# Attention ahead of a routed expert layer: Q and K in two buffers, 25 held tiles, loads spread out, gate transposes moved, last products in other banks

## The chip, the cores and the metric

The kernel runs on one core of one Trainium2 chip. The metric is the device time of one execution in microseconds; the numbers shown for a kernel are the median of several executions and their range. The core has a matrix engine (TensorE, PE in the profile; its weight loads are PEld), a vector engine (VectorE, DVE), a scalar engine (ScalarE, ACT), a general one (GpSimd, POOL) and a queue engine that issues transfers (SyncE, SP). Each engine runs its own instructions in the order in which the program was written and waits for the others through semaphores. Matrix products land in PSUM, eight banks; everything else lies in SBUF.

## The reference

Windowed attention with heads, and then a mixture of experts in which every expert takes exactly its share of the tokens:

```
B, H, S, D = 8, 8, 576, 64
scores = (q @ k.transpose(0, 1, 3, 2)) / sqrt(D)
mask = (rel >= 0) & (rel < 64)               # rel = row - column
scores = where(mask, scores, -1e9) - max
attn = exp(scores); attn /= attn.sum() + 1e-9
x = (attn @ v).transpose(0, 2, 1, 3).reshape(B * S, H * D)   # 4608 x 512
...
logits = x @ w_gate                          # 4608 x 8
for idx in argsort(-logits.flatten()):       # highest first
    token, expert = idx // 8, idx % 8        # token free and expert under 576: it goes there
...
out[mask] = relu(x[mask] @ w1[e]) @ w2[e]    # 512 -> 1024 -> 512 for each expert
```

## The kernel before, in words

There are three stages: attention (the first 157 us or so), the routing of the first expert (to about 183 us, a search on DVE and PE), and the experts, which fill PE to the end. All instructions behind the attention stand in the same order in both kernels; the change touches the function `attention` and nothing else.

The 4608 rows are worked through in 36 units of 128 rows, that is two blocks of 64 queries each. A batch has nine blocks, so units 0 to 4 touch batch 0, 4 to 8 batch 1, and batch b begins in unit 9b//2. Step s of the main loop (the last loop of the function) writes down, in this order: the score products of unit s (`qk`, L133, PE) and their masking and row maximum (L142, DVE, eight instructions), the subtraction of the maximum (L149, POOL); the transposes of unit s-1 (`tr`, L155, PE, two groups of four heads) and their exponentials (L157, ACT); the products with V of unit s-2 (`pv`, L176, PE), a small copy of the row sums (L206, ACT), and on DVE the reciprocal (L207), the gate logits (L191) and the values (L201) (`norm`). Whatever the table `at` holds for step s comes last.

That table holds the gate work. The logits x @ w_gate are not made from x: V @ w_gate is made for each batch in two parts (blocks 0 to 3 and 4 to 8) and appended to V as eight columns. For each part there are the gate products (`gate_mm`, L88, PE), the gate copy out of PSUM (`gate_cp`, L92, ACT), the gate transposes (`gate_tr`, L98, PE) and the copies into V (`gate_out`, L104 and L107, ACT). After that come the even copies (`even`, L119, ACT): V shifted by 64 rows, two instructions for each of four tiles of a batch, needed because a block of 64 queries sees 128 keys that may begin in the middle of a tile of V.

PSUM: scores have four tiles of one bank each (`SP`), `bank()` hands out two banks in turn to gate products, gate transposes and each group of score transposes, and products with V have two (`po`). So a group of score transposes waits until the bank that was handed out two turns earlier has been read by ACT.

SBUF and transfers: Q and K have three buffers each, V with its columns (`VO`) three, the transposed V (`VT`) and the shifted one (`VE`) two. SP issues the loads of batches 0 and 1 at once, and in step (9(b-2)+5)//2 those of batch b: VT, Q, K, V, in that order. A load waits for the last reader of its buffer. The values of a unit lie in a ring of HOLD + 4 tiles until they are stored to `xs` in HBM; HOLD (16) and LOADED say how many are held back, and from which step two go out per step.

Of the kernel before, what the change touches and what calls it, by code (L numbers as in the profile page):

```python
# [9 lines left out]
FT = mybir.dt.float32  # L10
# [11 lines left out]
HP = H // 2  # L22
E = 8
WARM = 30
VW = 73
DM = H * D
HOLD = 16
LOADED = 9 * (B - 3) + 12


def attention(ctx, tc, c, q, k, v, vt, gate, xs, L, choices, setup, counters):
# [9 lines left out]
    SP = [[ps.tile([128, 2, 128], FT, name=f"Sp{r}{i}", bufs=1) for i in range(2)] for r in range(2)]  # L41
# [22 lines left out]
    def load_qk(b, i0, i1, h=slice(0, HP), q2=nc.sync):  # L64
        if not i0 and not h.start:
            Q[b] = ld.tile([128, HP, S], FT, name="Q", bufs=3)
            K[b] = ld.tile([128, HP, S], FT, name="K", bufs=3)
        for q1, t, x in ((nc.sync, Q, q), (q2, K, k)):
            q1.dma_start(t[b][:, h, 64 * i0:64 * i1], x[b, h, :, 64 * i0:64 * i1].rearrange("h p s -> p h s"))
# [51 lines left out]
    PT_, ST, OP_ = {}, {}, {}  # L121

# [44 lines left out]
    def pv(m, g):  # L167
        Op = po.tile([128, 4, VW], FT, name="Op")
# [52 lines left out]
    def load_all(b):  # L221
        load_vt(b, *ALL)
        load_qk(b, *ALL)
        load_v(b, *ALL)

    n = 36
# [5 lines left out]
    for b in range(B):  # L232
        s0 = (9 * (b - 1) + (6 if b < 4 else 7)) // 2
        for i, s in zip(PARTS, ((0, 2), (3, 5))[b] if b < 2 else (s0, s0 + 2)):
            put(s, gate_mm, b, *i)
            put(s, gate_cp, b, *i)
            put(s + 1, gate_tr, b, *i)
            put(s + 1, gate_out, b, *i)
# [3 lines left out]
    for b in range(2, B):  # L242
        put((9 * (b - 2) + 5) // 2, load_all, b)
# [10 lines left out]

    for s in range(n + 2):
        if s < n:
            fs = [qk(s, g) for g in range(2)]
            for g in range(2):
# [4 lines left out]
                sm(s, g)  # L263
        if 1 <= s < n + 1:
            for g in range(2):
                tr(s - 1, g)
        if 2 <= s:
            for g in range(2):
                pv(s - 2, g)
            nrm = [norm(s - 2, g) for g in range(2)]  # L270
            for inv, gates, values in nrm:
                for f in (inv, gates, values) if s < n + 1 else (inv, gates):
                    f()
            if s >= n:
                while late:
                    late.pop(0)()
            if s == n + 1:
                for inv, gates, values in nrm:
                    values()
        for f, a in at.get(s, []):  # L280
            f(*a)
        for _ in range(1 if 2 * s < LOADED else 2):
            if stores and (len(stores) > HOLD or 2 * s > LOADED):
                store(*stores.pop(0))
# [786 lines left out]
```

## Time and profile before

| | |
|---|---|
| median of 3 executions | 658.53 us (658.21 to 661.87) |
| the profiled execution | 659.36 us, of which its span is 657.7 us |
| busy share of the span | PE 95%, PEld 81%, DVE 66%, ACT 51%, POOL 33% |
| attention, 36 units | scores of unit 0 begin at 6.10 us, of unit 35 at 148.50 us |

A row of the timeline gives the start and the length in microseconds, the engine, the line, the operation, the tile written and those read, the shape, and how many equal instructions were merged; behind it, in brackets, how long the engine had stood idle and which event ended that. PE rows overlap, since matrix products are pipelined: a busy PE is not a PE at its peak, and the start of the first row that follows tells when PE was through.

### The profile page before, as it was taken

Reading aid. Unit: us, or ns where it says so; the run is one execution under the profiler, and the core shown is the slowest. Engines: PE = TensorE matmul, PEld = TensorE weight load, DVE = VectorE, ACT = ScalarE, POOL = GpSimd, SP = SyncE. Lnnn points to the kernel's source line nnn. Section 1 sums busy time; section 2 is a strip of 40 time slices with the busy share of each in tenths; the row PEclk is TensorE's granted clock in tenths of the full one; section 3 lists DMA queues with packets and bytes.
Section 4 is the critical chain, followed back from the end, with each engine's and each line's share of the span. In section 5 each row is a group of like instructions: output and inputs, shape, how many; then the busy total and the mean of one; then the engine's idle time right before and its main releaser. Section 6 shows DMA issues by size and latency. Waiting matters only on the chain. (4 is left out here: it accounts for less than half of the span.)

```text
span 657.7 us, 16919 instructions
## 1 busy us (share of the span) xinstructions
PE 622.0 (95%) x6383; PEld 533.8 (81%) x6383; DVE 433.0 (66%) x2109; ACT 335.6 (51%) x602; POOL 219.2 (33%) x233
## 2 busy tenths in 40 slices
PE   7889999996489999999999999999999999999995
PEld 6667777775379878987997898899789879989984
DVE  5788888887787776875886687588668852202300
ACT  2586777783056157436715642672564266256310
POOL 3644545552051043206303320630342063052211
PEclk8999999998589999999999999999999999999998
DMA  9999989931087279739847972975798299939701
GB/s 302 339 366 375 353 286 377 380 142 67 18 279 154 41 266 232 159 106 268 200 87 259 232 164 94 269 197 102 252 223 182 70 289 257 233 106 215 145 24 48
DMA packets 50097, 134.10 MB, mean 204 GB/s; under 512 B 4696, under 2 KB 10968, under 8 KB 50016
## 3 DMA queue, kind: packets, MB, share of 16 engines
q0 software_dynamic: 15280, 52.98, 36.2%
q1 hardware_dynamic: 34192, 79.52, 33.8%
q8 instruction: 50, 0.82, 0.5%
q10 hardware_dynamic: 544, 0.52, 0.2%
q14 instruction: 31, 0.25, 0.1%
HBM read 82.15 MB, written 18.87 MB: 154 GB/s over the span
## 5 line engine op out<-in xcount | busy, mean ns | idle before, releaser
L951 POOL DMA_INDIRECT out<-ot,idx x40 | 40.8, 1021 | 296.4 <-DVE ab L629 98.4
L900 ACT ACTIVATE hh<-h 128x256 fp32r<-128x256 f32 (+1 forms) x128 | 52.1, 408 | 103.7 <-PE h L928 102.7
L971 PE MATMUL o<-wh,hl 128*128 128x512 f32 x256 | 102.2, 399 | 0.0
L971 PE MATMUL o<-wl,hh 128*128 128x512 f32 x256 | 102.0, 398 | 0.0
L971 PE MATMUL o<-wh,hh 128*128 128x512 f32 x256 | 100.4, 392 | 0.0
L149 POOL TENSOR_TENSOR st<-st,mx 128x512 f32<-128x512 f32 x72 | 73.4, 1040 | 73.7 <-DVE mx L142 54.2
L928 PE MATMUL h<-xh,wl 128*128 128x256 f32 (+1 forms) x512 | 94.4, 299 | 0.0
L928 PE MATMUL h<-xh,wh 128*128 128x256 f32 (+1 forms) x512 | 91.6, 299 | 0.7 <-ACT xh L856 0.7
L928 PE MATMUL h<-xl,wh 128*128 128x256 f32 (+1 forms) x512 | 91.1, 297 | 0.5 <-DVE xl L860 0.5
L905 DVE SCALAR_TENSOR_TENSOR hl<-h,hh 128x256 fp32r<-128x256 f32 x128 | 53.3, 416 | 42.4 <-ACT hh L900 42.0
L928 PEld LDWEIGHTS h<-xh,wh 128*128 128x128 f32 x512 | 75.6, 189 | 1.6 <-ACT xh L856 0.8
L928 PEld LDWEIGHTS h<-xh,wl 128*128 128x128 f32 x512 | 76.4, 189 | 0.2
L928 PEld LDWEIGHTS h<-xl,wh 128*128 128x128 f32 x512 | 75.5, 189 | 0.8 <-DVE xl L860 0.7
L142 DVE CUSTOM_DVE_ANT_0 st<-Sp,mask 128x128 f32<-128x128 f32 x288 | 67.4, 285 | 8.0 <-PE Sp L133 7.7
L811 ACT ACTIVATE wh<-st 128x1024 fp32r<-128x1024 f32 x64 | 67.2, 1050 | 3.3 <-DMA st<-w 3.0
L820 ACT ACTIVATE wl<-wh 128x1024 fp32r<-128x1024 f32 x61 | 64.5, 1057 | 1.2
L822 POOL DMA_DIRECT2D wl<-st x61 | 56.9, 1236 | 17.4 <-ACT wl L820 14.5
L971 PEld LDWEIGHTS o<-wl,hh 128*128 128x128 f32 x256 | 48.1, 188 | 9.3
L971 PEld LDWEIGHTS o<-wh,hh 128*128 128x128 f32 x256 | 48.2, 188 | 9.2
L971 PEld LDWEIGHTS o<-wh,hl 128*128 128x128 f32 x256 | 48.3, 189 | 8.8
L860 DVE TENSOR_TENSOR xl<-tp,xh 128x512 fp32r<-128x512 f32 (+1 forms) x40 | 25.0, 633 | 45.3 <-ACT xh L856 44.9
L866 POOL DMA_INDIRECT xg<-xs,idx x40 | 40.8, 1020 | 34.7 <-DVE eq L709 23.1
(178 smaller groups left out, 1088.4 us busy)
## 6 DMA issues: line engine op xcount, KB each, us to landing
wl<-st POOLq DMA_DIRECT2D x61, 512.0 KB
st<-w SPq DMA_DIRECT2D x60, 512.0 KB, 10.0
xs<-x SPq DMA_DIRECT2D x36, 256.0 KB, 8.0
VO<-v SPq DMA_DIRECT2D x6, 1168.0 KB, 17.8
VT<-vt SPq DMA_DIRECT2D x6, 1152.0 KB, 14.3
Q<-q SPq DMA_DIRECT2D x6, 1152.0 KB
K<-k SPq DMA_DIRECT2D x6, 1152.0 KB
VO<-v SPq DMA_DIRECT2D x4, 584.0 KB, 11.1
```

What stands on the lines that cost most here:

```text
L142: nc.vector.tensor_tensor_reduce(st[:, h, :], Sp[h % 2][:, h // 2], mk, scale=-0.125, scalar=3.0e38, op0=OP.add, op1=OP.min, accum_out=mx[ ...
L149: nc.gpsimd.tensor_tensor(st, st, mx[:, :, None].to_broadcast([128, 4, 128]), OP.subtract)
L811: nc.scalar.activation(hi, st[i], AF.Copy)
L820: nc.scalar.activation(lo, hi.bitcast(FT), AF.Copy, scale=-1.0)
L822: nc.gpsimd.dma_start(lo.bitcast(FT), st[i], accum_op=OP.add)
L860: nc.vector.tensor_tensor(xl[:, :, r], t[:, :, :n], xh[:, :, r].bitcast(FT), OP.subtract)
L866: nc.gpsimd.indirect_dma_start(out=g[0:n, a], out_offset=None, in_=self.xs, in_offset=IndirectOffsetOnAxis(ap=idx[0:n, a:a + 1], axis=0))
L900: nc.scalar.activation(hh[:, f, c0:c1], h, AF.Relu)
L905: nc.vector.scalar_tensor_tensor(t, h[:, a - c0:b - c0], 0.0, hh[:, f, a:b].bitcast(FT), op0=OP.max, op1=OP.subtract)
L928: nc.tensor.matmul(h, wv[:, cc, 128 * (f % 2):128 * (f % 2) + 128], xt[:, cc, c0:c1], start=(k == 0), stop=(k == 11))
L951: nc.gpsimd.indirect_dma_start(out=self.out, out_offset=IndirectOffsetOnAxis(ap=idx[0:m, a:a + 1], axis=0), in_=ot[0:m], in_offset=None)
L971: nc.tensor.matmul(o, ht[:, f, 128 * a:128 * a + 128], wt[:, 512 * (f % 2):512 * (f % 2) + 512], start=(k == 0), stop=(k == 23))
```

## The change

- Q and K get two buffers each instead of three, and the held values 29 tiles instead of 20 (HOLD 25).
- The loads of batch b are written down in three steps: VT 7 steps before the batch begins, V 6, Q and K 4 steps before. LOADED is 29.
- The gate products of a batch's two parts stand in steps f-1 and f, where f is the unit in which the batch begins (batch 0: 1 and 2, batch 1: 5 and 6, batch 7: f-3 and f-1). Before they stood two steps apart.
- The gate transposes and the copies into V, before at the end of the step after the products, now stand in that step between the scores and the score transposes.
- The even copies still stand at the end of the step after the products, and of the steps behind it.
- In step 36 the products with V of unit 34 come before the score transposes of unit 35, and land in two of the scores' banks.

```diff
-HOLD = 16
-LOADED = 9 * (B - 3) + 12
+HOLD = 25
+LOADED = 29
...
-    SP = [[ps.tile([128, 2, 128], FT, name=f"Sp{r}{i}", bufs=1) for i in range(2)] for r in range(2)]
+    SB = [[ps.tile([128, 512], FT, name=f"Sp{r}{i}", bufs=1) for i in range(2)] for r in range(2)]
+    SP = [[x[:, 0:256].rearrange("p (h k) -> p h k", h=2) for x in y] for y in SB]
...
-            Q[b] = ld.tile([128, HP, S], FT, name="Q", bufs=3)
-            K[b] = ld.tile([128, HP, S], FT, name="K", bufs=3)
+            Q[b] = ld.tile([128, HP, S], FT, name="Q")
+            K[b] = ld.tile([128, HP, S], FT, name="K")
...
     def pv(m, g):
-        Op = po.tile([128, 4, VW], FT, name="Op")
+        if m == n - 2:
+            Op = SB[g][0][:, 0:4 * VW].rearrange("p (h w) -> p h w", h=4)
+        else:
+            Op = po.tile([128, 4, VW], FT, name="Op")
...
     for b in range(B):
-        s0 = (9 * (b - 1) + (6 if b < 4 else 7)) // 2
-        for i, s in zip(PARTS, ((0, 2), (3, 5))[b] if b < 2 else (s0, s0 + 2)):
+        f = 9 * b // 2
+        for i, s in zip(PARTS, {0: (1, 2), 1: (5, 6), B - 1: (f - 3, f - 1)}.get(b, (f - 1, f))):
             put(s, gate_mm, b, *i)
             put(s, gate_cp, b, *i)
-            put(s + 1, gate_tr, b, *i)
-            put(s + 1, gate_out, b, *i)
+            put(s + 0.5, gate_tr, b, *i)
+            put(s + 0.5, gate_out, b, *i)
             for j in range(4):
                 if i[0] <= 2 * j + 2 < i[1]:
                     put(s + 1 + max(0, j - 1), even, b, j, not b and j < 2)
     for b in range(2, B):
-        put((9 * (b - 2) + 5) // 2, load_all, b)
+        f = 9 * b // 2
+        put(f - 7, load_vt, b, *ALL)
+        put(f - 6, load_v, b, *ALL)
+        put(f - 4, load_qk, b, *ALL)
...
+        for f, a in at.get(s - 0.5, []):
+            f(*a)
+        if s == n:
+            quotients(s)
         if 1 <= s < n + 1:
             for g in range(2):
                 tr(s - 1, g)
-        if 2 <= s:
...
+        if 2 <= s and s != n:
+            quotients(s)
```

`quotients(s)` holds what stood in the loop for unit s-2: `pv`, `norm`, and behind step 35 the rest of the routing's preparations.

On ACT, in steps 21 to 23 (the gate work of batch 5), the kernel before has these rows, from the even copies at the end of step 21 on (L119 even copies, L92 gate copy, L104 and L107 copies into V, L157 exponentials, L206 row sums):

```order
L119 ACTIVATE VE<-VO 64x584 x2
L92 ACTIVATE vs<-Tp 128x256
L157 ACTIVATE pt<-Tp 128x512 x2
L206 ACTIVATE r<-Op 128x4 x2
L119 ACTIVATE VE<-VO 64x584 x2
L104 ACTIVATE VO<-Tp 128x16x8
L119 ACTIVATE VE<-VO 64x584 x2
L157 ACTIVATE pt<-Tp 128x512 x2
L206 ACTIVATE r<-Op 128x4 x2
L92 ACTIVATE vs<-Tp 128x320
```

The same place in the changed kernel, where the lines are L120, L93, L105, L108, L159 and L211:

```order
L120 ACTIVATE VE<-VO 64x584 x2
L93 ACTIVATE vs<-Tp 128x256
L105 ACTIVATE VO<-Tp 128x16x8
L159 ACTIVATE pt<-Tp 128x512 x2
L211 ACTIVATE r<-Op 128x4 x2
L120 ACTIVATE VE<-VO 64x584 x2
L93 ACTIVATE vs<-Tp 128x320
L105 ACTIVATE VO<-Tp 128x16x8
L108 ACTIVATE VO<-Tp 64x8x8
L159 ACTIVATE pt<-Tp 128x512 x2
```

Before, even copies of two tiles (batch 4's last, batch 5's first) stand around one copy into V; now each step has the even copies of one tile, the gate copy behind them, and the copies into V right behind that, ahead of the exponentials.

On PE, the kernel before has the gate transposes of batch 5's second part (L98) behind the products with V of step 24 and ahead of the next unit's score products (L133):

```order
L176 MATMUL Op<-VE,pt 64x73
L176 MATMUL Op<-VO,pt 64x73
L98 MATMUL Tp<-ident,vs 128x128 x2
L98 MATMUL Tp<-ident,vs 64x128
L133 MATMUL Sp_95<-K,Q 64x128
```

In the changed kernel the same transposes (L99) stand in step 23, behind the score products (L135) and ahead of the score transposes (L157):

```order
L135 MATMUL Sp_96<-K,Q 64x128
L135 MATMUL Sp_98<-K,Q 64x128
L99 MATMUL Tp<-ident,vs 128x128 x2
L99 MATMUL Tp<-ident,vs 64x128
L157 MATMUL Tp<-ident,st 128x128 x8
L181 MATMUL Op<-VE,pt 64x73
```

Between the gate products and their transposes PE had the score products, the score transposes and the products with V of a step; it now has the score products alone.

On SP, the loads of batch 2 before:

```order
L62 DMA VT<-vt 128x4x576
L69 DMA Q<-q 128x4x576
L69 DMA K<-k 128x4x576
L75 DMA VO<-v 128x4x584
L78 DMA VO<-v 64x584
```

and now:

```order
L63 DMA VT<-vt 128x4x576
L76 DMA VO<-v 128x4x584
L79 DMA VO<-v 64x584
L70 DMA Q<-q 128x4x576
L70 DMA K<-k 128x4x576
```

Each later batch has the same order, and all 36 stores now stand behind the last load of K; before, seven of them stood ahead of the last batch's loads.

## Rows read from the trace of the kernel before

**Rows 1.** Busy time by stretch: its bounds in us, its length, then PE, PEld, DVE, ACT and POOL busy (instructions), the granted TensorE clock, the share of the DMA engines and GB/s.

```profile
46.50:80.00 33.50, 31.13 (x626) 25.06 (x628) 26.88 (x194) 24.06 (x57) 16.41 (x17) 1.00 1.01 364
115.00:150.00 35.00, 34.73 (x714) 27.49 (x711) 29.87 (x218) 27.15 (x64) 18.51 (x19) 1.00 0.68 252
```

**Rows 2.** The waits of DVE between 26 and 150 us: who waited, for whom, us in total, times, the longest.

```profile
DVE r L207 <- ACT r L206: 9.9, 16, 2.2
```

**Rows 3.** Timeline of DVE: the first of the eight score instructions of units 10, 19, 20, 21, 22, 23, 24 and 35, and one reduction of the logits (L195, once in four units).

```profile
51.61 0.29 DVE L142 CUSTOM_DVE_ANT_0 st<-Sp,mask 128x128 f32<-128x128 f32 x1
...
85.95 0.28 DVE L142 CUSTOM_DVE_ANT_0 st<-Sp,mask 128x128 f32<-128x128 f32 x1
89.82 0.29 DVE L142 CUSTOM_DVE_ANT_0 st<-Sp,mask 128x128 f32<-128x128 f32 x1 [0.18 <-PE Sp L133]
93.53 0.29 DVE L142 CUSTOM_DVE_ANT_0 st<-Sp,mask 128x128 f32<-128x128 f32 x1
97.05 0.62 DVE L195 TENSOR_REDUCE L<-l 128x32 f32<-128x256 f32 x1
97.92 0.28 DVE L142 CUSTOM_DVE_ANT_0 st<-Sp,mask 128x128 f32<-128x128 f32 x1
101.25 0.28 DVE L142 CUSTOM_DVE_ANT_0 st<-Sp,mask 128x128 f32<-128x128 f32 x1
106.02 0.28 DVE L142 CUSTOM_DVE_ANT_0 st<-Sp,mask 128x128 f32<-128x128 f32 x1
148.50 0.28 DVE L142 CUSTOM_DVE_ANT_0 st<-Sp,mask 128x128 f32<-128x128 f32 x1
```

**Rows 4.** Timeline of ACT in steps 20 to 23.

```profile
92.81 0.29 ACT L104 ACTIVATE VO<-Tp 128x128 f32<-128x128 f32 x1 [0.29 <-PE Tp L98]
92.98 0.21 ACT L107 ACTIVATE VO<-Tp 64x64 f32<-64x64 f32 x1
93.22 1.40 ACT L119 ACTIVATE VE<-VO 64x584 f32<-64x584 f32 x2
...
96.06 0.17 ACT L206 ACTIVATE r<-Op 128x4 f32<-128x4 f32 x1 [0.26 <-PE Op L176]
96.25 1.39 ACT L119 ACTIVATE VE<-VO 64x584 f32<-64x584 f32 x2
97.67 0.38 ACT L92 ACTIVATE vs<-Tp 128x256 f32<-128x256 f32 x1
...
100.24 1.40 ACT L119 ACTIVATE VE<-VO 64x584 f32<-64x584 f32 x2
101.67 0.29 ACT L104 ACTIVATE VO<-Tp 128x128 f32<-128x128 f32 x1
101.99 1.39 ACT L119 ACTIVATE VE<-VO 64x584 f32<-64x584 f32 x2
103.40 1.08 ACT L157 ACTIVATE pt<-Tp 128x512 f32<-128x512 f32 x2
```

**Rows 5.** Timeline of PE in steps 20 to 22: gate transposes at the end of step 20, score transposes of step 21, gate products at the end of step 21, score transposes of step 22.

```profile
92.22 0.55 PE L98 MATMUL Tp<-ident,vs 128*128 128x128 f32 x3
93.74 1.10 PE L155 MATMUL Tp<-ident,st 128*128 128x128 f32 x8
95.94 0.64 PE L88 MATMUL Tp<-VT,wgs 128*32 128x256 f32 x8
97.54 1.28 PE L155 MATMUL Tp<-ident,st 128*128 128x128 f32 x8
```

**Rows 6.** Timeline of DVE: the three longest waits for the row sums behind 26 us.

```profile
49.44 0.18 DVE L207 RECIPROCAL r<-r 128x4 f32<-128x4 f32 x1 [2.20 <-ACT r L206]
...
104.58 0.18 DVE L207 RECIPROCAL r<-r 128x4 f32<-128x4 f32 x1 [1.36 <-ACT r L206]
...
139.89 0.18 DVE L207 RECIPROCAL r<-r 128x4 f32<-128x4 f32 x1 [1.45 <-ACT r L206]
```

**Rows 7.** Around the landing of batch 2's V: timeline of ACT (the first row) and of PE; and from the list of DMA issues the loads of V, with KB each and the median us from issue to landing.

```profile
46.52 0.29 ACT L104 ACTIVATE VO<-Tp 128x128 f32<-128x128 f32 x1 [0.69 <-DMA VO<-v]
```

```profile
46.96 0.63 PE L155 MATMUL Tp<-ident,st 128*128 128x128 f32 x4 [0.78 <-ACT VO L104]
```

```profile
VO<-v SPq DMA_DIRECT2D x6, 1168.0 KB, 17.8
```

**Rows 8.** Timeline of PE: two stops in the middle of a unit's score products; and the queue that carries instructions (packets, MB, share of the DMA engines).

```profile
62.68 1.03 PE L133 MATMUL Sp<-K,Q 64*64 64x128 f32 x26 [0.84 <-issue]
...
113.19 0.54 PE L133 MATMUL Sp<-K,Q 64*64 64x128 f32 x9 [0.64 <-issue]
```

```profile
q8 instruction: 50, 0.82, 0.5%
```

**Rows 9.** The end of the attention: timeline of PE (score transposes of unit 35 in two groups, and the first product with V behind a wait), then of DVE (last reciprocal, and the last instruction ahead of the routing).

```profile
150.90 0.66 PE L155 MATMUL Tp<-ident,st 128*128 128x128 f32 x4 [0.48 <-POOL st L149]
151.89 0.66 PE L155 MATMUL Tp<-ident,st 128*128 128x128 f32 x4 [0.34 <-POOL st L149]
154.42 0.25 PE L176 MATMUL Op<-VO,pt 128*64 128x73 f32 x1 [0.69 <-DVE r L207]
```

```profile
156.65 0.18 DVE L207 RECIPROCAL r<-r 128x4 f32<-128x4 f32 x1 [0.42 <-ACT r L206]
...
158.49 0.19 DVE L454 TENSOR_TENSOR one<-w,best 128x32 bf16<-128x32 bf16 x1
```

More of the change, by code (lines that the diff above doesn't have):

```diff
@@ L121, in attention @@
     PT_, ST, OP_ = {}, {}, {}
+    n = 36
     def qk(m, g):
@@ L219, in attention @@
             load_v(b, *i)
[L221 to L226, printed above, removed]
     at = {}
@@ L253, in small, with quotients @@
                 next(setup, None)
+    def quotients(s):
+        for g in range(2):
+            pv(s - 2, g)
+        nrm = [norm(s - 2, g) for g in range(2)]
+        for inv, gates, values in nrm:
+            for f in (inv, gates, values) if s < n + 1 else (inv, gates):
+                f()
+        if s >= n:
+            while late:
+                late.pop(0)()
+        if s == n + 1:
+            for inv, gates, values in nrm:
+                values()
     for s in range(n + 2):
@@ L266, in attention @@
                 tr(s - 1, g)
-        if 2 <= s:
[L268 to L279, printed above, removed]
+        if 2 <= s and s != n:
+            quotients(s)
         for f, a in at.get(s, []):
             f(*a)
-        for _ in range(1 if 2 * s < LOADED else 2):
-            if stores and (len(stores) > HOLD or 2 * s > LOADED):
+        for _ in range(1 if s < LOADED else 2):
+            if stores and (len(stores) > HOLD or s > LOADED):
                 store(*stores.pop(0))
```

## The prediction

> **What bounds the kernel now.** Only the attention's order changes, so the question is by how much its end moves; routing and experts behind it keep their order and move with it. I read the busy times by stretch first. Up to 80 us the DMA engines are taken up entirely (share 1.01, 364 GB/s), behind 115 us they are not (0.68), and PE is busy in nearly all of both [rows 1]. PE rows overlap, so the second view is the waits of DVE, which closes each unit: between 26 and 150 us it waits 9.9 us for the row sums from ACT [rows 2], and three waits make up half of that [rows 6]. The third view is the spacing of the units' first scores, a step in what follows [rows 3]:
>
> - 3.33 us without gate work on PE (units 22 to 23, 97.92 to 101.25);
> - 3.86 with gate products at its end (85.95 to 89.82), 3.71 with them at its start (89.82 to 93.53);
> - about 0.6 more where the logits are reduced (97.05, 0.62 us);
> - 4.77 where ACT is behind (101.25 to 106.02). There four even copies and a copy into V stand ahead of the exponentials, which begin at 103.40, and the row sums stand behind the exponentials [rows 4].
>
> So no engine alone is the bound: a step is a loop over PE (score products, score transposes, products with V), ACT (exponentials, row sums) and DVE (scores, values), with almost no slack, and what delays ACT's exponentials delays the step.
>
> **What the change removes.** The stacks of four even copies at the ends of steps 4, 8, 22 and 31 come apart. The waits of 1.36 and 1.45 us belong to the last two [rows 6]: -2.8 us. The first two lie ahead of 50 us, where something else decides (below). A new stack of two tiles' even copies arises in step 9, and one in step 29.
>
> **What it adds: the gate transposes' two waits.** A gate transpose that waits holds up the score transposes behind it on PE, as the wait at 46.96 held up what followed [rows 7]. I count from the start of the gate products. In step 21 they start at 95.94, the score transposes behind the next score products at 97.54, 1.60 us later [rows 5]. ACT meanwhile does the row sums (96.06), two even copies (96.25, 1.39 us) and only then the gate copy, 97.67 to 98.05, 2.11 us after the start [rows 4]. Before, half of the score transposes went ahead of that. Now the gate transposes need the copy, and start at 2.2 instead of 1.6: wait one, 0.6 us. Wait two: the second group of score transposes takes the bank of the gate transposes and so needs the copies into V. These ended 0.97 us after the start of the transposes (92.22 to 93.19) [rows 4, 5]; with a tenth for the signal the second group starts 1.1 us behind, where it started half of 1.10 us behind the first [rows 5]. It is this second wait that the row at 46.96 shows once in the kernel before, for 0.78 us [rows 7]. Together the second group, its exponentials, the row sums and the values come 0.6 + 1.1 - 0.55 = 1.15 us later, and 3.71 becomes 4.86; DVE is free a little earlier than PE, so I take 4.8. The part ahead of it, with products at its end: 3.86 + 0.6 + 0.35 (two transposes, one copy) = 4.8 too when even copies stand ahead of its gate copy, 4.2 when none do.
>
> From unit 10 to 35 there are 25 steps. By the new table:
>
> - 8 at 4.8: second parts in steps 14, 19, 23, 28, 31; first parts in 13, 22, 29, with the previous batch's even copies ahead: 38.4;
> - 2 first parts without them (18, 27) at 4.2: 8.4;
> - step 10, behind the stack of step 9 and the copy: four even copies of 0.7 and the copy of 0.44 end 3.55 us after the start, 1.4 us behind the case above, less what the reduction in step 9 hides: 6.0;
> - step 30, a stack without copies into V: 4.77 less those 0.3: 4.4;
> - 2 with products at the end only (12, 26) at 3.86: 7.7;
> - 4 with a reduction (17, 21, 25, 33) at 3.33 + 0.6: 15.8;
> - 7 others at 3.33: 23.3.
>
> Sum 104.0 us, where the kernel before took 148.50 - 51.61 = 96.9 [rows 3]: +7.1. That holds the removal of the last two stacks already.
>
> **What it moves: the loads.** Up to unit 9 the bytes decide. V of batch 2 lands at 46.52, last of all bytes of three batches [rows 7], with the DMA engines full [rows 1]. Now V goes ahead and K comes last, at the same time, for the bytes are the same. Before, unit 9's scores were done when the wait ended; now its score products begin with it. Behind 46.5 come score products (1.0), gate transposes and score transposes with the second wait (1.6), products with V (1.1), gate products (0.7) and half of unit 10's score products (0.6) and a signal: scores of unit 10 at about 51.9, +0.3. The earlier stacks, and the wait of 2.20 us, vanish in that wait, so I book nothing for them. Two buffers for Q and K: the load of batch b waits for the score products four steps ahead of its first use, some 15 us, and 2.36 MB take 6.5 us at 364 GB/s [rows 1] behind an empty queue; I take nothing. If they took what V took, 17.8 us [rows 7], each of four batches would lose 3 us; that is a rival. Stores: SP has no other work behind the last load (about 118 us), 36 stores of 256 KB are 9.4 MB or 26 us at that rate, and the ring of 29 lets unit 29 wait only for the first store. Nothing; if the ring did block, 8 us is the upper end, and the last store would then hold up the first gathers.
>
> **The end.** Unit 35's score transposes wait for POOL until 150.90 and 151.89, and unit 34's products with V stand behind them; then unit 35's wait for a bank until 154.42 [rows 9]. Now unit 34's products begin where PE began to wait, at 150.4, and run 1.1 us to 151.6 while POOL works, the transposes follow to 152.6, exponentials to 153.2, and unit 35's products, whose banks unit 33 has left by then, end at 153.9. The last reciprocal comes at 154.5 instead of 156.65; what follows to 158.49 [rows 9] stays: -2.1 us. Bounds: 0 if DVE gets no earlier through unit 34, -2.5 if the reciprocal follows at once.
>
> **Sum:** +7.1 + 0.3 - 2.1 = +5.3 us. On the profiled execution's 659.36 us that is 664.7; the median stands 0.8 lower, at 658.53, so 663.8.
>
> Two stops of PE inside score products, 0.84 and 0.64 us with no semaphore behind them, lie in the 96.9 us and not in my 104.0 [rows 8]. [...]
>
> **The rivals.**
>
> *An even trade, 657 us.* The gate copy gets through before the score products end, and only the reordering on PE counts: 4.2 instead of 4.8 in eight steps (-4.8) and in step 10 (-1.8), 663.8 - 6.6 = 657.2. For it: without even copies ahead only the row sums stand in front of the copy, and two first parts have that. Against it: at 98.05 it was 0.5 us behind [rows 4, 5]. It decides at a copy that ends within 1.6 us of the products' start. [...]
>
> *Faster, 651 us.* The rearrangement hides all that ACT does: the three long waits go (2.20 + 1.36 + 1.45 = 5.0 us) [rows 6], nothing takes their place, and the end gives 2.1: 651.4. For it: these are DVE's largest waits. Against it: each new step has copies on both sides of the gate transposes. It decides if steps with gate work stay under 3.9 us.
>
> *Slower by late Q and K, 671 us or more.* Two buffers make each load wait for the last reader; landing takes over 15 us, and PE stands in front of the score products of units 18, 22, 27 and 31. At 17.8 us [rows 7] it is 4 x 3 = 12 us, less what that wait hides of the gate steps (about 5): 671. For it: loads of this size took that long while queued behind others. Against it: the queue is not full then [rows 1].
>
> *No effect.* That the change does nothing is out: order and buffers are another program, but the even trade is close to it.
>
> **How the numbers follow.** The forecast (660 to 668) has 0.55, the even trade 0.20, the faster case 0.11, late loads 0.14. One per cent, 6.6 us, is about what a measurement of this kernel tells from no change. Of the forecast's 0.55 some 0.37 lie under 665.1 and 0.18 above; with the even trade and a little of the faster case, same is 0.58; faster 0.10; slower 0.18 + 0.14 = 0.32. The range goes from 654 (between even trade and faster case) to 669 (ahead of the late loads), which leaves out about 0.1 on each side; the forecast's own range is 660 to 668.
>
> **What would show it.** Score starts 4.8 us apart in steps 13, 14, 19, 22, 23, 28, 29 and 31; PE waiting for ACT's gate copy ahead of the gate transposes and for its copies into V ahead of score transposes; about 6 us in step 10; unit 9's score products waiting for K until 46 to 47 us; PE never waiting for Q or K behind that; the last reciprocal 8 us behind unit 35's first scores before, 6 now. I am wrong if those steps stay near 4, or if PE waits for loads behind 60 us.

## The result, and the profile after

The changed kernel takes 664.65 us (median of 4, 664.0 to 665.61) beside 658.91 us of the kernel before: a ratio of 1.0081 with a 95% interval of 1.0052 to 1.011. By that ratio it is +5.3 us (the two medians are 5.7 apart); the forecast was 663.8 us. The profiled execution has a span of 662.6 us, where the one before had 657.7.

First the waits, grouped: who waited, for whom, us in total, times, the longest. PE between 46 and 150 us in the changed kernel:

```profile
PE Tp L99 <- ACT vs L93: 5.8, 9, 1.9
PE Sp L135 <- issue: 1.3, 1, 1.3
PE Sp L135 <- DMA K<-k: 1.0, 1, 1.0
```

and DVE between 26 and 150 us:

```profile
DVE r L212 <- ACT r L211: 17.3, 17, 3.2
DVE st L144 <- PE Sp L135: 1.8, 5, 1.1
```

The gate transposes wait nine times for the gate copy, a wait that the kernel before did not have, and DVE's waits for row sums grew from 9.9 us [rows 2] to 17.3. The stretch from unit 10's first scores to unit 35's took 156.42 - 52.12 = 104.3 us, where it was 96.9 [rows 3]: +7.4. The forecast for it was 104.0. PE waits for K once, at unit 9, and for no load behind that.

The two windows of waits are not that stretch. Inside it, these are DVE's waits of the kernel before (two rows) and of the changed one, and then the busy times of the stretch in the same order (length, then PE, PEld, DVE, ACT and POOL busy, granted clock, DMA share, GB/s):

```profile
DVE r L207 <- ACT r L206: 6.6, 13, 1.5
DVE st L142 <- PE Sp L133: 1.6, 4, 1.0
...
DVE r L212 <- ACT r L211: 15.2, 15, 3.2
DVE st L144 <- PE Sp L135: 0.7, 4, 0.2
```

```profile
51.61:148.50 96.89, 94.75 (x1916) 75.44 (x1912) 82.81 (x596) 72.84 (x171) 50.91 (x50) 1.00 0.87 315
...
52.12:156.42 104.30, 96.33 (x1912) 77.09 (x1912) 82.72 (x596) 77.83 (x176) 50.98 (x50) 0.98 0.81 290
```

DVE is busy for 82.8 and 82.7 us: its own work is the same. What the change costs there is time in which DVE waits, 8.6 us more for the row sums and 0.9 less for score products.

The timeline of DVE, first scores of units 10, 13, 14, 15, 19, 20, 21, 22, 23, 24 and 35:

```profile
52.12 0.28 DVE L144 CUSTOM_DVE_ANT_0 st<-Sp,mask 128x128 f32<-128x128 f32 x1
...
66.05 0.29 DVE L144 CUSTOM_DVE_ANT_0 st<-Sp,mask 128x128 f32<-128x128 f32 x1
71.36 0.28 DVE L144 CUSTOM_DVE_ANT_0 st<-Sp,mask 128x128 f32<-128x128 f32 x1
75.72 0.28 DVE L144 CUSTOM_DVE_ANT_0 st<-Sp,mask 128x128 f32<-128x128 f32 x1
...
90.36 0.29 DVE L144 CUSTOM_DVE_ANT_0 st<-Sp,mask 128x128 f32<-128x128 f32 x1 [0.18 <-PE Sp L135]
95.12 0.28 DVE L144 CUSTOM_DVE_ANT_0 st<-Sp,mask 128x128 f32<-128x128 f32 x1
98.43 0.28 DVE L144 CUSTOM_DVE_ANT_0 st<-Sp,mask 128x128 f32<-128x128 f32 x1
102.25 0.27 DVE L144 CUSTOM_DVE_ANT_0 st<-Sp,mask 128x128 f32<-128x128 f32 x1
106.65 0.29 DVE L144 CUSTOM_DVE_ANT_0 st<-Sp,mask 128x128 f32<-128x128 f32 x1 [0.17 <-PE Sp L135]
111.42 0.28 DVE L144 CUSTOM_DVE_ANT_0 st<-Sp,mask 128x128 f32<-128x128 f32 x1
...
156.42 0.28 DVE L144 CUSTOM_DVE_ANT_0 st<-Sp,mask 128x128 f32<-128x128 f32 x1
```

Step 20 is a light step, 3.31 us (95.12 to 98.43). Steps 19, 22 and 23 with gate work take 4.76, 4.40 and 4.77; step 13, which has a reduction besides, 5.31. What fills such a step stands in the timelines of PE and ACT for steps 21 to 23:

```profile
100.34 0.64 PE L89 MATMUL Tp<-VT,wgs 128*32 128x256 f32 x8
100.91 1.10 PE L135 MATMUL Sp<-K,Q 64*64 64x128 f32 x32
102.51 0.44 PE L99 MATMUL Tp<-ident,vs 128*128 128x128 f32 x2 [0.49 <-ACT vs L93]
102.79 1.26 PE L157 MATMUL Tp<-ident,st 128*128 128x128 f32 x8
...
107.37 0.55 PE L99 MATMUL Tp<-ident,vs 128*128 128x128 f32 x3 [0.44 <-ACT vs L93]
```

```profile
100.66 1.39 ACT L120 ACTIVATE VE<-VO 64x584 f32<-64x584 f32 x2
102.08 0.38 ACT L93 ACTIVATE vs<-Tp 128x256 f32<-128x256 f32 x1
102.99 0.29 ACT L105 ACTIVATE VO<-Tp 128x128 f32<-128x128 f32 x1 [0.53 <-PE Tp L99]
103.48 1.26 ACT L159 ACTIVATE pt<-Tp 128x512 f32<-128x512 f32 x2 [0.21 <-PE Tp L157]
```

PE is through with the score products at 102.0 and stands until ACT has done two even copies and the gate copy (102.46). Then ACT stands for the transposes, does the copy into V, and begins the exponentials at 103.48, 3.1 us after the gate products began. All of the first wait is on PE, all of the second on ACT: each engine is idle while the other is at one short piece of the gate work.

Step 10 took 6.94 us, the largest miss in a single step (forecast 6.0). Its rows of ACT and PE, and the table by stretch (length, PE, PEld, DVE, ACT and POOL busy, granted clock, DMA share, GB/s):

```profile
50.53 2.81 ACT L120 ACTIVATE VE<-VO 64x584 f32<-64x584 f32 x4
53.36 0.44 ACT L93 ACTIVATE vs<-Tp 128x320 f32<-128x320 f32 x1
```

```profile
53.85 0.55 PE L99 MATMUL Tp<-ident,vs 128*128 128x128 f32 x3 [1.86 <-ACT vs L93]
```

```profile
54.00:55.00 1.00, 0.92 (x8) 0.71 (x8) 0.12 (x2) 0.52 (x3) 1.00 (x2) 1.00 1.00 369
55.00:56.00 1.00, 1.00 (x6) 0.67 (x8) 0.00 (x0) 0.52 (x2) 0.48 (x1) 0.51 1.06 392
56.00:57.00 1.00, 1.00 (x19) 1.00 (x21) 0.00 (x0) 0.55 (x1) 0.00 (x0) 0.50 1.06 392
57.00:58.00 1.00, 1.00 (x19) 0.85 (x16) 0.56 (x3) 0.17 (x1) 0.00 (x0) 0.50 1.04 387
58.00:59.00 1.00, 1.00 (x30) 1.00 (x32) 0.70 (x4) 0.84 (x2) 0.00 (x0) 0.78 1.07 396
```

The stack of four even copies ahead of the gate copy was foreseen, and the wait of 1.86 us. What was not: about 1.2 us behind it the granted clock falls from 1.00 to 0.50 for 3.4 us (55.03 to 58.44). The products with V that fall into that time take 1.88 us from the start of the first to the start of the last (55.85 to 57.73), where those of the step before took 1.02 (49.03 to 50.05): 0.86 us, nearly the whole miss.

The loads and the end, in the timelines of PE and DVE (K of batch 2, the one stop without a semaphore, the last reciprocal, the last instruction ahead of the routing):

```profile
46.53 0.62 PE L135 MATMUL Sp<-K,Q 64*64 64x128 f32 x13 [1.01 <-DMA K<-k]
...
118.64 0.76 PE L135 MATMUL Sp<-K,Q 64*64 64x128 f32 x17 [1.33 <-issue]
```

```profile
162.40 0.17 DVE L212 RECIPROCAL r<-r 128x4 f32<-128x4 f32 x1
...
164.22 0.19 DVE L463 TENSOR_TENSOR one<-w,best 128x32 bf16<-128x32 bf16 x1
```

Unit 9's score products begin with the landing of K; unit 10's first scores come at 52.12 instead of 51.61, +0.5. The last reciprocal stands 162.40 - 156.42 = 6.0 us behind unit 35's first scores, where it was 8.15 [rows 3, 9]: -2.2. So +0.5 + 7.4 - 2.2 = +5.7 us at the end of the attention, +5.3 in the time, and +4.9 in the spans of the two profiled executions.

### The profile page after: what moved, and what is told of

The parts are those of the page before. It is cut to its first block, busy times and chain, and to the rows that moved or that the text cites. A ratio compares the mean times of both kernels' runs of the same rounds, so it can differ in the third digit from the quotient of the medians.

```text
span 662.6 us, 16976 instructions
## 1 busy us (share of the span) xinstructions
PE 623.0 (94%) x6383; PEld 535.7 (81%) x6383; DVE 433.4 (65%) x2109; ACT 338.9 (51%) x602; POOL 220.8 (33%) x233
## 5 line engine op out<-in xcount | busy, mean ns | idle before, releaser
L909 ACT ACTIVATE hh<-h 128x256 fp32r<-128x256 f32 (+1 forms) x128 | 52.2, 409 | 103.7 <-PE h L937 102.7
L980 PE MATMUL o<-wl,hh 128*128 128x512 f32 x256 | 102.0, 398 | 0.0
L937 PE MATMUL h<-xh,wl 128*128 128x256 f32 (+1 forms) x512 | 94.4, 299 | 0.0
L914 DVE SCALAR_TENSOR_TENSOR hl<-h,hh 128x256 fp32r<-128x256 f32 x128 | 53.3, 417 | 42.2 <-ACT hh L909 42.0
```

Source lines behind the costliest of these rows:

```text
L909: nc.scalar.activation(hh[:, f, c0:c1], h, AF.Relu)
L914: nc.vector.scalar_tensor_tensor(t, h[:, a - c0:b - c0], 0.0, hh[:, f, a:b].bitcast(FT), op0=OP.max, op1=OP.subtract)
L937: nc.tensor.matmul(h, wv[:, cc, 128 * (f % 2):128 * (f % 2) + 128], xt[:, cc, c0:c1], start=(k == 0), stop=(k == 11))
L980: nc.tensor.matmul(o, ht[:, f, 128 * a:128 * a + 128], wt[:, 512 * (f % 2):512 * (f % 2) + 512], start=(k == 0), stop=(k == 23))
```

## The experiments

The theory: the gate transposes' place ahead of the score transposes makes PE wait for ACT and ACT for PE, and that is what costs the time. The rivals: ACT's even copies and its other copies are too much in such a step in whatever order; the gate products' new steps; the loads. All runs are timed against the kernel before on the same chip (659.91, 659.10 and 660.07 us in the three series). S10 and S35 are the first scores of units 10 and 35, "end" is the last reciprocal behind S35, "stops" is PE's standing still for over 0.1 us without a semaphore between S10 and S35, all in us from the traces. In b_cp_first 2.4 of the 2.6 us are waits for a bank (below). The changed kernel's own interval is 1.9 us to either side, so the times alone do not tell a difference of some 2 us to it from none; S10 to S35 comes from one trace of each kernel, and a stop or a fallen clock in it counts too.

| kernel | median us | ratio to before, 95% interval | S10 | S10 to S35 | end | stops |
|---|---|---|---|---|---|---|
| before | | 1 | 51.6 | 96.9 | 8.2 | 1.6 |
| changed | 664.65 | 1.0081 (1.0052 to 1.011) | 52.1 | 104.3 | 6.0 | 1.3 |
| g_tr_behind | 661.58 | 1.0024 (1.001 to 1.0038) | 52.7 | 100.6 | 6.0 | 1.8 |
| b_cp_first | 663.26 | 1.005 (1.003 to 1.0069) | 53.0 | 101.6 | 6.0 | 2.6 |
| a_tr_end | 661.04 | 1.0023 (1.0009 to 1.0036) | 51.8 | 100.8 | 6.0 | 2.4 |
| p_pool | 660.13 | 1.0012 (0.9999 to 1.0025) | 52.2 | 99.7 | 6.0 | 3.5 |
| e_end | 658.26 | 0.9973 (0.9959 to 0.9987) | 51.4 | 97.1 | 6.5 | 1.8 |
| l_loads | 659.22 | 1.0007 (0.999 to 1.0023) | 51.8 | 96.6 | 8.1 | 1.8 |
| m_move | 666.04 | 1.0098 (1.0078 to 1.0119) | 55.5 | 100.3 | 8.1 | 2.3 |
| m_loads | 669.4 | 1.0134 (1.0109 to 1.0159) | 54.2 | 105.2 | 8.1 | 4.2 |
| f_end_shift | 656.51 | 0.9954 (0.9935 to 0.9973) | 51.1 | 95.4 | 6.5 | 1.1 |
| f_b2_late | 658.85 | 0.999 (0.9971 to 1.0009) | 52.4 | 96.5 | 6.5 | 1.4 |
| f_pool | 655.63 | 0.9934 (0.9911 to 0.9958) | 50.8 | 95.6 | 6.2 | 1.5 |
| f_all | 655.26 | 0.9929 (0.9904 to 0.9954) | 52.3 | 95.3 | 6.2 | 0.8 |

### From the changed kernel: undoing one thing at a time

**g_tr_behind.** The lines that write the gate transposes stand behind those of the score transposes:

```diff
-        for f, a in at.get(s - 0.5, []):
-            f(*a)
         if s == n:
             quotients(s)
         if 1 <= s < n + 1:
             for g in range(2):
                 tr(s - 1, g)
+        for f, a in at.get(s - 0.5, []):
+            f(*a)
```

> The changed kernel with one edit: the gate transposes and the copies into V stand behind both groups of score transposes of their step, ahead of the products with V, instead of ahead of the score transposes. Theory of the prediction (the transposes' place on PE: they wait for ACT's gate copy, and hold the score transposes and so the exponentials behind them): the nine waits for the gate copy, 5.8 us in the trace of the changed kernel, go, and the exponentials no longer stand behind the copies into V; of the 17.3 us that DVE waits for row sums about 6 go, and the time falls from 664.7 to 658 to 660. Rival (ACT's total work in a step sets it, in whatever order): within 1 us of 664.7. Rival (the loads): within 1 us of 664.7 too, and PE would be seen waiting for Q or K.

Measured 1.0024, that is 3.8 us less than the changed kernel's 1.0081; the gate transposes no longer wait for the gate copy. So the place matters, but less than the 5 to 6 us expected: DVE still waits 14.0 us for row sums. Two of the 3.7 us that S10 to S35 loses lie in steps 10 and 11 (6.94 and 3.60 us in the changed kernel, 5.14 and 3.33 here). The wait behind the stack in step 10 is not gone there. It has moved to the second group of score transposes, whose bank the gate products had before, and is shorter; the clock stays at 1.00:

```profile
54.54 0.63 PE L157 MATMUL Tp<-ident,st 128*128 128x128 f32 x4 [1.37 <-ACT vs L93]
```

**b_cp_first.** The even copies move behind the gate copy of the same step:

```diff
-                    put(s + 1 + max(0, j - 1), even, b, j, not b and j < 2)
+                    put(s + 1.25 + max(0, j - 1), even, b, j, not b and j < 2)
...
-        for f, a in at.get(s, []):
-            f(*a)
+        for t in (s, s + 0.25):
+            for f, a in at.get(t, []):
+                f(*a)
```

> The changed kernel with one edit: on ACT the gate copy stands ahead of the even copies of its step. Theory of the prediction: PE's waits for the gate copy (0.44 to 0.5 us in a usual part, 1.86 in step 10) vanish, but the copies into V and the exponentials still stand behind the even copies; in step 22 the exponentials could begin at 103.1 instead of 103.5, so 0.3 to 0.4 us for each of nine parts and about 0.5 in step 10: 664.7 - 3 = 661 to 662. If PE's wait alone were the cost: -5.8, 659. If the copy's place does not matter: 664 to 665.

Measured 1.005: -2.0 us, where 3 were expected. The intervals overlap, so the times alone do not show that this edit gains anything; the trace has S10 to S35 shorter by 2.7 us. The 5.8 us of PE's wait alone did not come off. With wait one gone, the other comes into the open. PE in step 19 of this kernel (gate transposes, then the two groups of score transposes):

```profile
91.36 0.55 PE L99 MATMUL Tp<-ident,vs 128*128 128x128 f32 x3
91.74 0.60 PE L157 MATMUL Tp<-ident,st 128*128 128x128 f32 x4
92.82 0.63 PE L157 MATMUL Tp<-ident,st 128*128 128x128 f32 x4 [0.48 <-issue]
```

The second group stands until ACT has emptied the gate transposes' bank. The copies into V ended at 92.72, behind the even copies, 0.1 us before it starts; the wait is marked "issue", since the trace shows no event for it. That it is the bank is read from this and from the order of the banks. In step 10, behind four even copies, the same wait is 1.89 us long, and its row names POOL, which was done with that unit at 51.0:

```profile
55.66 0.63 PE L157 MATMUL Tp<-ident,st 128*128 128x128 f32 x4 [1.89 <-POOL st L151]
```

The granted clock is 0.50 from 56.5 to 59.9 us here too, and steps 10 and 11 take 10.49 us together, as in the changed kernel (10.54). So in the worst place this edit gained nothing: it exchanged one wait for the other.

**a_tr_end.** Transposes and copies into V back at the end of the step behind their products. In this kernel the gate columns of the first units of batches 0 and 1 are written behind the products that read them, so the logits of those units are not the reference's (all of that lies ahead of unit 10):

```diff
-            put(s + 0.5, gate_tr, b, *i)
-            put(s + 0.5, gate_out, b, *i)
+            put(s + 1, gate_tr, b, *i)
+            put(s + 1, gate_out, b, *i)
```

> The changed kernel with the gate transposes and the copies into V back at the end of the step behind their products, as before; gate products, even copies, loads and the end stay as changed. Beside the kernel before the changed one stands at 1.008 (+5.3 us). Theory (the transposes' new place is the larger cost): 1.002 or less of the kernel before, +1 us or less, with no PE wait for the gate copy longer than 0.2 us, since score transposes and products with V stand in between. Rival (the gate products' new steps, one behind the other with even copies in front of both gate copies, are the larger cost): 1.005 or more, +3.5 us or more, the waits of DVE for row sums staying near 14 us.

Measured 1.0023, -3.8 us, in between. The place is worth 104.3 - 100.8 = 3.5 us of S10 to S35, but 100.8 is still 3.9 more than before, with the new steps of the products and of the even copies (the loads add nothing to that stretch in l_loads, the new end little in e_end). Without the stops of the three kernels it is some 4.5 us for the place and 3.2 for the new steps. So both cost several us, and the runs do not rank them. Step 10 still took 5.22 us here, behind the stack of step 9, and against the expectation PE still waited for the gate copy, three times and for 1.3 us in that step.

**p_pool.** The second even copy of each tile on POOL:

```diff
-            if early:
+            if d.start:
+                nc.gpsimd.tensor_copy(*a)
+            elif early:
```

> The changed kernel with the second even copy of each tile on POOL instead of ACT (some 0.7 us of ACT's work less wherever even copies stand). Theory (ACT's queue ahead of the gate copy and the exponentials makes the waits): the waits of PE for the gate copy (5.8 us) nearly all go, 0.7 us less in each of nine parts and in the stacks of steps 9 and 29, and the time falls from +5.3 to about -1 beside the kernel before (0.998), if POOL's subtraction is not delayed by more than that. Rival (PE's own order and work is the cost, not what ACT does ahead): within 1 us of +5.3. Other side: POOL's copies delay the subtraction ahead of the score transposes, and PE waits for POOL: above +5.3.

Measured 1.0012: -4.5 us, short of the expected -6 but the most that a single edit gave, and 99.7 us holds 3.5 of stops. The rival that ACT's work ahead does not matter is out. PE's waits for the gate copy are gone, and no wait of PE for POOL appears. From the groups by line, POOL between 46 and 150 us (busy us, mean ns of one, idle before):

```profile
L118 POOL COPY VE<-VO 64x584 f32<-64x584 f32 x26 | 17.2, 665 | 1.5
```

A copy takes POOL 665 ns, where one on ACT took 688 ns in m_move, and fits between the subtractions, which fill 52.0 of these 104 us.

### From the kernel before: one part of the change alone

**e_end**: the new end (the parts of the diff on `SB`, `pv` and `quotients`), nothing else.

```diff
...
+        if s == n:
+            quotients(s)
         if 1 <= s < n + 1:
...
-        if 2 <= s:
...
+        if 2 <= s and s != n:
+            quotients(s)
```

> The kernel before with the new end alone: in step 36 unit 34's products with V come before unit 35's score transposes and land in two of the scores' banks. The prediction's term: -2.1 us (bounds 0 and -2.5), so 656.8 beside 658.9; the last reciprocal 6.0 us behind unit 35's first scores instead of 8.15. Rival (what is gained at the end is given back in the routing or the experts): the last reciprocal is earlier, but the time stays within 0.5 us of the kernel before.

Measured 0.9973 (0.9959 to 0.9987), -1.8 us, and 1.7 at the last reciprocal: the term holds, a little smaller, and nothing is given back.

**l_loads**: buffers, HOLD, LOADED and the loads' steps.

```diff
...
-        put((9 * (b - 2) + 5) // 2, load_all, b)
+        f = 9 * b // 2
+        put(f - 7, load_vt, b, *ALL)
+        put(f - 6, load_v, b, *ALL)
+        put(f - 4, load_qk, b, *ALL)
...
```

> The kernel before with the new buffers and loads alone: two buffers for Q and K, 29 value tiles, loads of a batch written down 7, 6 and 4 steps ahead, stores behind the last load. The prediction's term: +0.3 us (K of batch 2 lands at 46 to 47 us and unit 9's score products wait for it; no wait for Q or K behind 50 us), so 659.2 beside 658.9. Rival of late loads: PE waits in front of the score products of units 18, 22, 27 and 31, 3 us each: 668 or more.

Measured 1.0007 (0.999 to 1.0023): no difference that can be measured. Of PE's waits between 26 and 150 us, the only one for a load:

```profile
PE Sp L133 <- DMA K<-k: 1.7, 1, 1.7
```

One wait, at unit 9, as forecast; with two buffers no later load of Q or K is late. That rival is out.

**m_move**: only the place of the gate transposes and copies into V.

```diff
-            put(s + 1, gate_tr, b, *i)
-            put(s + 1, gate_out, b, *i)
+            put(s + 0.5, gate_tr, b, *i)
+            put(s + 0.5, gate_out, b, *i)
...
+        for f, a in at.get(s - 0.5, []):
+            f(*a)
         if 1 <= s < n + 1:
```

> The kernel before with one edit: the gate transposes and the copies into V ahead of the score transposes of the step behind their products; products, even copies, loads and end as before. In the old table no even copies stand ahead of the gate copy of a second part, so wait one (0.45 us) comes only in five first parts, and the hold of the score transposes and exponentials behind transposes and copies, 0.3 us, in ten: 5 x 0.45 + 10 x 0.3 = 5.2 at most, less the time that the same transposes no longer take at the end of a step's products (they stand there for 0.28 to 0.4 us each either way): theory +2 to +4 us, 1.003 to 1.006. Rival (the place costs only together with the new steps): +1 us or less.

Measured 1.0098, +6.5 us, more than the 2 to 4 expected. S10 to S35 grew by 3.4 us, within the 2 to 4; the rest came ahead of it, and I had not seen it. ACT and PE in step 8:

```profile
45.90 0.29 ACT L104 ACTIVATE VO<-Tp 128x128 f32<-128x128 f32 x1 [2.96 <-DMA VO<-v]
```

```profile
46.33 0.66 PE L155 MATMUL Tp<-ident,st 128*128 128x128 f32 x4 [2.46 <-POOL st L149]
```

The copy into V of batch 2 needs V, which lands last of its batch. At the end of a step only the even copies stood behind that wait [rows 7]; now all exponentials of the step do, and unit 10 begins 3.9 us later. PE's row names POOL, which was done with that unit at 42.2: by the order of the banks the second group of score transposes waits for the gate transposes' bank, and so for ACT.

**m_loads**: m_move and l_loads together.

> The kernel before with two parts of the change: the gate transposes and copies into V ahead of the score transposes, as in m_move, and the new buffers and loads, as in l_loads. In m_move ACT stood 2.96 us in front of the copy into V of batch 2 (V landed at 45.9), with the exponentials behind it, and unit 10's scores came at 55.5 instead of 51.6. Theory (V, last of its batch in the old order, takes 3.9 of m_move's 6.5 us; ahead of Q and K it lands some 6 us earlier): that wait goes, unit 9's score products wait for K instead, unit 10's scores come at 52 to 53, and the time is 1.005 to 1.007 of the kernel before. Rival (the place alone costs 6.5 us in the old table): 1.009 or more.

Measured 1.0134, worse than either and against the expectation. V does land in time (no wait for it is left), but S10 only falls to 54.2, and S10 to S35 grows to 105.2. Stops of PE take 4.2 us of it, and 2.8 between 44 and 52 us. The longest, in PE's timeline, and the stretches behind it:

```profile
74.77 0.29 PE L176 MATMUL Op<-VO,pt 128*64 128x73 f32 x2 [2.08 <-issue]
```

```profile
75.00:76.00 1.00, 1.00 (x25) 0.63 (x23) 0.60 (x3) 0.35 (x2) 0.18 (x1) 1.00 0.10 37
76.00:77.00 1.00, 1.00 (x24) 0.77 (x20) 0.71 (x4) 0.44 (x1) 0.00 (x0) 0.61 0.13 30
77.00:78.00 1.00, 1.00 (x24) 0.82 (x16) 0.47 (x5) 0.00 (x0) 0.00 (x0) 0.50 0.72 62
```

A stop of 2.08 us, and again a clock of 0.50 behind it: steps 14 and 15 take 5.70 and 5.10 us, 3.7 more than in m_move. That is most of the 4.9 us by which the stretch is longer. Why the stops were longer here than in m_move or l_loads stays open.

### Toward a better kernel

**f_end_shift**: e_end, and the last even copies of batches 4 and 6 a step later.

```diff
-                    put(s + 1 + max(0, j - 1), even, b, j, not b and j < 2)
+                    put(s + 1 + max(0, j - 1) + (j == 3 and b in (4, 6)), even, b, j, not b and j < 2)
```

> The kernel before with the new end, and the last even copies of batches 4 and 6 one step later, so that the stacks of four even copies in steps 22 and 31 come apart. The prediction's term for these stacks: -2.8 us, with the end's -1.8 as measured: 0.993 of the kernel before. Rival (the work on ACT only moves to the next step, ahead of its gate copy): steps 22 and 23 together and 31 and 32 together become shorter by 0.9 us each or less, 0.994 to 0.997.

Measured 0.9954, 0.0019 or 1.3 us less than e_end (the intervals overlap). The two long waits [rows 6] are gone, but of each 1.0 us that steps 23 and 32 lost (4.77 to 3.78, 4.85 to 3.86) the next step took back 0.5 to 0.6 (3.60 to 4.08, 3.84 to 4.44): 0.9 us are left in the four steps. The rival was right: the work moved.

**f_b2_late**: f_end_shift with batch 2's gate work one step later.

```diff
-        for i, s in zip(PARTS, ((0, 2), (3, 5))[b] if b < 2 else (s0, s0 + 2)):
+        for i, s in zip(PARTS, ((0, 2), (3, 5), (8, 10))[b] if b < 3 else (s0, s0 + 2)):
...
-                    put(s + 1 + max(0, j - 1) + (j == 3 and b in (4, 6)), even, b, j, not b and j < 2)
+                    put(s + 1 + max(0, j - 1) + (j == 3 and b in (2, 4, 6)), even, b, j, not b and j < 2)
```

> The kernel of f_end_shift with the gate work of batch 2 one step later (products in steps 8 and 10 instead of 7 and 9, transposes at the end of the step behind, the last even copies of batch 2 another step later). Theory (step 9's 6.1 us come from ACT waiting for V, which lands at 46): the wait falls behind the exponentials of unit 9, step 9 takes about 4, and 1.5 to 2 us come off: 0.992 to 0.993 of the kernel before. Rival (up to 80 us the bytes decide, and what is saved here is lost at the next load): within 0.5 us of f_end_shift's 0.9954.

Measured 0.999: slower than f_end_shift, against the theory, and step 9 took 6.1 us again. ACT's wait for V is gone, but in PE's timeline stands

```profile
50.30 0.28 PE L181 MATMUL Op<-VO,pt 128*64 128x73 f32 x1 [1.58 <-issue]
```

a stop in the products with V of step 9, where f_end_shift has one of 0.61 us (48.68). Besides, unit 9 began 1.3 us later here already, and step 12 is 0.7 us longer. Why the stop is longer the trace does not say.

**f_pool** and **f_all**: f_end_shift and f_b2_late, each with p_pool's edit.

> The kernel of f_end_shift with the second even copy of each tile on POOL. Theory (ACT's queue is what the waits of DVE come from, 8.0 us of them left in f_end_shift): 1 to 2 us less, 0.992 to 0.994. Rival (in the old table ACT is no longer late, PE is the bound): 0.995 to 0.996. Other side (POOL's copies hold up its subtractions, and PE waits for those): above 0.997.

> The kernel of f_b2_late with the second even copy of each tile on POOL, the two together. If the two gains are of different waits they add: 0.990 to 0.992. If both shorten the same step 9 or PE is the bound by then: no better than the better of the two alone.

Measured 0.9934 and 0.9929, not told apart: 4.4 to 4.7 us less than the kernel before and some 10 less than the changed one. In f_pool the even copies on POOL bring 1.3 us over f_end_shift, inside the overlap of the intervals, so no gain is shown; DVE's waits for row sums between 26 and 150 us are 7.5 us, with 7.6 in f_end_shift. So with the stacks apart, ACT's even copies are no longer what DVE waits for in the old table. These two beat both kernels.

## Why the prediction was right, step by step

- **The sum.** +0.5 +7.4 -2.2 against +0.3 +7.1 -2.1. Two terms were also measured alone: the end -1.8 (e_end), the loads +0.5 (l_loads, -0.7 to +1.5 by its interval). The loads' own terms add up to 46.5 + 5.0 = 51.5 us and a signal (from the end of the gate copy to the gate transposes behind it 0.05 us, 102.46 to 102.51), and hardly to 51.9. PE kept to them: unit 10's score products began at 50.89. Its first scores came at 52.12, since DVE, which had waited for row sums until 50.02, was at unit 7's logits, their reduction and the values until then. That this small term came out is luck.
- **The eight steps at 4.8.** They took 5.31 (13), 4.36 (14), 4.76 (19), 4.40 (22), 4.77 (23), 4.92 (28), 5.34 (29) and 4.58 (31): together 38.4, as forecast. It is partly luck. Steps 13 and 29 hold a reduction that my list left out there; without one the steps took 4.36 to 4.92.
- **Wait one**, forecast 0.6: 0.44 to 0.51 in seven of nine, 0.72 in step 31. Right in kind, a little large.
- **Wait two**, forecast as 0.55 us in a second part and 0.35 in a first: right in size, but not for the most part a wait. The second group of score transposes starts 1.07 us behind the gate transposes in step 23 (107.37 to 108.44) and 0.91 in step 22 (102.51 to 103.42); less the 0.55 of the forecast that is 0.52 and 0.36. Of this, 0.39 and 0.28 are PE's own work on the gate transposes. The second group starts 0.68 and 0.63 us behind the first, where 0.49 is usual (step 20), so the wait for the bank is 0.15 to 0.2. ACT is idle when the transposes end, so its copy overlaps the first group. In b_cp_first it is 0.48.
- **The step that the waits were added to** was misread, and so part of the agreement is luck. The 3.71 us of step 20 before were put down to gate products at its start; these were over before unit 20's first scores (89.82), and what the step holds are three gate transposes at its end (92.22 [rows 5]). So the transposes' own time is counted twice, in the 3.71 and in wait two. Nor is step 22 before, with 3.33 us, free of gate work. In the timeline of PE, the kernel before:

```profile
88.31 0.74 PE L88 MATMUL Tp<-VT,wgs 128*32 128x320 f32 x8
...
99.93 0.44 PE L98 MATMUL Tp<-ident,vs 128*128 128x128 f32 x2
```

- **A light step** is DVE's own work: in steps 15, 20, 24, 32 and 34 of the changed kernel (3.31 to 3.33 us) DVE never waits for over 0.15 us. The prediction had no single engine as the bound. Steps 19 and 23 are 1.45 us longer than that, 1.35 of it DVE's wait for row sums, where the forecast added 1.15 to 3.71: too large a base, and too small a delay.
- **Step 10**, forecast 6.0: 6.94. The wait was foreseen, the fallen clock was not.
- **The stacks**, -2.8 us of "what the change removes": mis-sized. f_end_shift against e_end gives 1.3 in the time (the intervals overlap) and 0.9 in the four steps, and the work moved on to the next steps.
- **What carries the +7.1.** The text laid it on the two waits of the gate transposes. The runs divide it: 3.5 us for their place (a_tr_end against the changed kernel, and 3.4 in m_move against the kernel before), 3.9 for the products' new steps. Without the stops the place is 4.5 us in the new table and 2.7 in the old, and the new steps 3.2; some 0.9 of the place's 4.5 is the fallen clock in step 10. By my own list (3.8 us for a gate step, 5.2 for step 10) a_tr_end would have had 104.0 - 8.0 - 0.8 - 0.8 = 94.4 us, and it has 100.8. Of the 6.4 us, 2.4 are stops, about 1.2 (at the forecast's own 0.6) the reductions of steps 13 and 29, and 2.3 lie in five steps that the list has at 3.33 (11, 15, 20, 24 and 32: 3.70 to 4.02). So what failed is the attribution: the list had no price for the steps behind a second part. In step 20 of a_tr_end the copies into V (92.01) and two even copies (92.42) stand ahead of the exponentials (93.85), whose transposes began at 92.94. The likely reason for the rest: steps of gate work at 3.71 and 3.86 belonged to a table with a free step between a batch's two parts. With the parts side by side, copy into V, even copies and gate copy stand one behind the other on ACT in the same step, and p_pool, which lightens only ACT, takes back 4.5 us.
- **PE's stops.** The 104.0 us hold none, with two of 0.84 and 0.64 us in the rows of before [rows 8]. One came in the changed kernel's stretch too: 1.33 us (step 26, 4.39 us where the forecast had 3.86), beside 1.6 before in all, and up to 4.2 in a run here (m_loads).
- **The rivals.** Even trade: out, the gate copy is late in nine of twelve parts. Faster: out, the largest waits of before went, and more came. Late Q and K: out by l_loads.

## What to carry to other kernels

Work that shuttles between two engines (products, copy, transposes, copy) cost little here where a step of other work lay between its stages (3.33 and 3.34 us in steps 18 and 30 of the kernel before), and cost both engines where the stages stood back to back ahead of a critical instruction, with bulk copies in between in the queue of one of them (4.40 to 4.77 us in steps 19, 22 and 23 of the changed kernel, 3.31 in step 20). Before moving a stage forward, list all that will stand behind it in its queues and what it waits for itself, transfers too: m_move had lost 3.9 us by unit 10, behind V's landing, and 3.4 in all the steps from there. Look for an engine with idle time for the bulk copies before reordering the busy ones: with the second copy of each tile on POOL the changed kernel took 4.5 us less (p_pool). And find the engine that sets a step in which nothing waits, here DVE with 3.3 us: in the kernel before, gate transposes (step 18) and gate products (step 30) on PE left the step at 3.33 and 3.34 us, as if they were free, while the time that the change lost is time in which DVE waited.

## What the runs showed of the hardware

**PE's stops recur at the same counts.** Counted through PE's rows in each trace (loads of weights and sequencer rows too, each stop within one of the number), the stops of over 0.2 us without a semaphore, up to unit 35, fall on rows 450, 707, 963, 1219, 1475, 1731, 1987, 2243, 2499, 2755, 3011, 4035, 4291, 4546 and 4803 of the fourteen kernels: multiples of 256 apart, whatever the kernel does there. Exceptions are a short one at row 233 and those of 0.48 us in b_cp_first, which are waits for a bank. Not every kernel stops at each, and the lengths at one count differ (at 1475: 0.61 in f_end_shift, 0.95 before, 1.58 in f_b2_late, 2.28 in f_all). The instruction queue of the kernel before moved 0.82 MB in 50 packets [rows 8], 16.4 KB each. What a stop waits for, and whether it has to do with that queue, no event in the traces shows. The DMA engines were not full at one of the long ones: that of 1.33 us in the changed kernel (118.64) lies in a stretch, 115 to 120 us, with a DMA share of 0.29.

**The clock behind a pause.** PE stood 1.86 us in the changed kernel (until 53.85), 1.89 in b_cp_first (55.66), 2.08 in m_loads (74.77) and 2.46 in m_move (46.33), and each time the granted clock was 0.50 from 0.5 to 1.5 us later on, for 3.4 us. Pauses of 2.28 us in f_all (50.07), of 2.11 in a_tr_end (46.67) and of 2.07 in f_pool (46.98) left it at 1.00. So length alone does not decide it, and what does stays open; in the changed kernel it added some 0.9 us to a wait of 1.86.
